# Lightning attention, then a Mish MLP, on one core: reordering the head, the k scalings and chunk 11's loads

## The chip, the cores and the metric

The kernel runs on one core of one Trainium2 chip. The metric is the device time of one execution in microseconds; a kernel's time is the median of several runs. The kernel before took 213.41 us, the median of three runs from 212.65 to 213.62. A smaller time is better. Chip engines are named as in the profile: PE is TensorE (PEld its weight loads), DVE VectorE, ACT ScalarE, POOL GpSimd, SP SyncE, which here only issues DMAs.

## The reference

Linear attention with a decay per head, in blocks of 64 positions, then a two-layer MLP whose activation is Mish, h * tanh(softplus(h)):

```python
# q, k, v: (4, 8, 768, 64); lam: (8,), 0.97 to 0.99
Dmask = np.where(rel >= 0, lam[:, None, None] ** rel[None, :, :], 0.0)
for b in range(nb):                       # 12 blocks of 64 positions
    intra = np.einsum('bhic,bhjc->bhij', qb, kb) * Dmask[None]
    intra = np.einsum('bhij,bhjd->bhid', intra, vb)
    inter = np.einsum('bhid,bhde->bhie', qb * lam_pow[None], kv_state)
    out[:, :, sl] = intra + inter
    kv_state = lam_block[None, :, None, None] * kv_state + np.einsum('bhsd,bhse->bhde', kb * rev_pow[None], vb)
x = out.transpose(0, 2, 1, 3).reshape(3072, 512)
h = x @ w_in                              # 512 -> 2048
g = h * np.tanh(softplus(h))
return g @ w_out                          # 2048 -> 512, fp32
```

## The kernel before

**Tiling.** The kernel works in chunks of 128 positions of one batch entry with all 8 heads: 6 positions times 4 entries make 24 chunks, numbered 0 to 23; a *group* is the four chunks of one position, so group n is chunks 4n to 4n+3 and 512 rows of the MLP. Heads stand in pairs j (0 to 3) with t = 0, 1 inside a pair. All matmuls take fp16 operands.

**A chunk's attention in groups 0 and 1.** `first_t` transposes k and q on TensorE (`pk`, `pq`, four matmuls each) and copies them to SBUF: `pkT` by ScalarE, `pqT` by VectorE. `first_s` makes the scores of the 8 heads (`pS`, eight matmuls into two tiles, t = 0 and 1), and VectorE multiplies each of the two tiles by its decay mask (`dm` in group 0, `maskT` in group 1) into `sb`. `first_o` multiplies `sb` by v (`pO`, eight matmuls; group 1 adds four with the state `wst`), and ScalarE copies the result into `xt`, the MLP's input for the group. Chunks of group 1 use k scaled by its decay, `ktil` (`scale_k`: VectorE in group 0 and the last group, GpSimd in the others), and q scaled by `lq`, which four exponentials of ScalarE make (`q_decays`). `wst` is cleared by `clear` and filled by `state_half` (`pv`, two chunks at a time).

**Groups 2 to 5.** k and q are transposed by DMA: `turn` scales k on GpSimd, and SyncE issues two DMA transposes, `qraw` and `kraw`. Two chunks at a time, `pair_s` makes the scores and the state's part of the outputs, `pair_o` the rest, and SyncE transposes the result (`xtok`) into `xt`. `pair_a` updates the state; the decay of the state (`wc`, L304) runs on GpSimd.

**The MLP.** First layer: `mm1_unit` makes 128 of the 2048 columns for all 512 rows of a group (four matmuls of 128x512, then Mish on ScalarE); in group 1 `mm1_tile` does 512 columns for one chunk at a time, so that it can follow the chunks. Second layer: `mm2_unit` is a quarter of the 2048 terms for one chunk, four matmuls of 128x512; every fourth is copied out of PSUM by ScalarE and stored. Called a *unit* below: four such matmuls.

**What sets the order.** The schedule is written out by hand: every engine runs its instructions in the order in which the code issues them, and semaphores hold them until their data are there. Tables named `steps` say after which unit a piece of attention is put in. The stages are: the head (setup and group 0's chunks, with fillers `busy`, matmuls on zeros); group 0's first layer, unit by unit, with chunk 4 and 5's attention put in; group 1's first layer by tiles `(chunk, s)`; then, for groups 0 and 1 together, 32 units of the second layer with group 2's pairs put in; then for each group 16 units of the first layer and 16 of the second.

**Loads.** q, k, v of chunks 1 to 23 and the weights are loaded by GpSimd's queue, fp32 to fp16, in the order of the code. From group 3 on they are held back behind a `tick` on GpSimd, a copy of one element that waits for a given output. GpSimd's own arithmetic stands in the same queue.

**PSUM.** `pk`, `pq`, `pO` and the first half of `pS` have one buffer each; `po` (also the second half of `pS`, and `pv`) and `ph` (also `busy`) have two.

Of the kernel before, what the change touches and what calls it, by code (L numbers as in the profile page):

```python
# [8 lines left out]
F16 = mybir.dt.float16  # L9
AF = mybir.ActivationFunctionType  # L10
ALU = mybir.AluOpType
# [9 lines left out]
def kernel(  # L21
# [183 lines left out]
    def first_t(c, m=0):  # L205

        out_ = []
        first = c < B
        for src, name in ((k0 if c == 0 else kn[c] if first else ktil[c], "pk"),
                          (q0 if c == 0 else qn[c], "pq")):  # L210
            pt = ps.tile([128, JP, C], F16, name=name, tag=name)
            for j in range(JP):
                nc.tensor.matmul(  # L213
                    pt[:, j, :], src[:, 2 * j : 2 * j + 2, :].rearrange("p h c -> p (h c)"), ident,
                    is_transpose=True, start=(j == 0), stop=(j == JP - 1),
                )
            out_.append(work.tile([128, JP, C], F16, name=f"{name}T", tag=f"{name}T", bufs=2))
            if name == "pk":
                nc.scalar.activation(out_[-1], pt, AF.Copy)
                busy(m)  # L220
            elif first:
                nc.vector.tensor_copy(out_[-1], pt)
            else:
                nc.vector.tensor_tensor(out=out_[-1], in0=pt, in1=lq, op=ALU.mult)
        kq[c] = out_

    def first_s(c):

        kT, qT = kq[c]
# [5 lines left out]
        sb0[c] = []  # L235
        for t in range(2):
            sb0[c].append(work.tile([128, JP, C], F16, name="sb", tag="sb", bufs=4))
            nc.vector.tensor_tensor(out=sb0[c][t], in0=pS[t],  # L238
                                    in1=dm[:, t] if c < B else bc(maskT, 1, JP), op=ALU.mult)

    def first_o(c):
# [13 lines left out]
        nc.scalar.activation(xt[n][:, :, b * C : (b + 1) * C], psO, AF.Copy)  # L255
# [201 lines left out]
    first_t(0, 2)  # L457
# [16 lines left out]
    nc.scalar.preload_act_table(AF.Mish)  # L474
    first_o(1)
    first_s(2)
    busy(3)
# [136 lines left out]
```

## Time and profile before

| what | value |
|---|---|
| median of three runs | 213.41 us (212.65 to 213.62) |
| the profiled execution's own time | 213.85 us |
| its span, first to last instruction | 212.1 us |
| TensorE busy | 203.5 us, 96% of the span |
| ScalarE, VectorE, GpSimd busy | 86.7, 67.6, 100.0 us |
| DMA on GpSimd's queue (loads) | 13.37 MB, 85.2% of the time of 16 engines |
| DMA on SyncE's queue (transposes) | 6.63 MB, 20.4% |

A row of the timeline has its start, its length, the engine, the line, the operation, the tiles (out<-in) and the count of instructions merged in it; in brackets stands the engine's idle time before it and what ended that. A row about DMA to landing gives the shortest, median and longest time from issue to the data's arrival. The chain is followed back from the last instruction, at each step to what released it. Ends of matmuls are modelled, so the length of a row of matmuls holds the last one's way through the array.

### The profile page before, as it was taken

What the parts mean: (1) busy time and instruction counts of PE and PEld (TensorE: products, weight loads), DVE (VectorE), ACT (ScalarE), POOL (GpSimd) and SP (SyncE); (2) the same over time, 40 slices, a digit from 0 to 9 for tenths busy, and PEclk for the clock granted to TensorE, in tenths of its full rate; (3) what the DMA queues carried; (4) which work ended last, traced back from release to release, by engine and by line L of the source; (5) the groups of instructions that cost most, each with busy time, mean ns of one, the idle gap of its engine ahead of it and who ended that gap; (6) DMA issues with size and microseconds to landing.
All of it is one profiled execution on the core that took longest, in us unless ns stands there. A gap on an engine that the chain in (4) does not pass through costs nothing.

```text
span 212.1 us, 4293 instructions
## 1 busy us (share of the span) xinstructions
PE 203.5 (96%) x1758; PEld 110.5 (52%) x1758; DVE 67.6 (32%) x124; ACT 86.7 (41%) x150; POOL 100.0 (47%) x143
## 2 busy tenths in 40 slices
PE   7989898999999899999999999999999999999994
PEld 4655446999745454445554454544444544444442
DVE  7686613725004442042440042482042510000000
ACT  4764575655421112346412356312456321566120
POOL 7997389932996348786965067921000000000000
PEclk9999999999999999999999999999999999999999
DMA  9999999999999999999997799997702032100112
GB/s 129 133 157 185 189 156 99 172 189 164 121 145 195 185 182 164 163 189 153 156 166 148 182 87 84 144 166 141 190 9 49 5 99 104 49 0 0 49 53 99
DMA packets 109895, 26.78 MB, mean 126 GB/s; under 512 B 102578, under 2 KB 106930, under 8 KB 109874
## 3 DMA queue, kind: packets, MB, share of 16 engines
q0 software_dynamic: 78080, 13.37, 85.2%
q1 hardware_dynamic: 27296, 6.63, 20.4%
q10 hardware_dynamic: 4498, 6.49, 9.9%
q8 instruction: 14, 0.23, 0.5%
q14 instruction: 7, 0.06, 0.1%
HBM read 27.26 MB, written 6.29 MB: 158 GB/s over the span
## 4 chain that ended last, share of the span: by engine, by line
PE 82%; DMA 9%; DVE 2%; ACT 1%; POOL 1%; issue 1%; SPq 1%; POOLq 0%; ACTq 0%; DVEq 0%
PE po L412 33%; PE ph L380 30%; DMA kraw<-ktil 7%; PE ph L398 7%; PE pO L253 2%; PE pS L324 2%; DMA kn<-in_k_dram 2%; PE pO L351 2%; PE pS L234 1%; PE pv L288 1%; PE pk L213 1%; SPq L272 1%; PE busy L167 1%; PE pq L213 1%; POOL vz L79 1%
## 5 line engine op out<-in xcount | busy, mean ns | idle before, releaser
L412 PE MATMUL po<-wout,hsg 128*128 128x512 f16 (+2 forms) x400 | 85.4, 371 | 0.0
L380 PE MATMUL ph<-xt,win 128*128 128x512 f16 (+2 forms) x328 | 73.0, 374 | 0.5 <-ACT xt L255 0.3
L387 ACT ACTIVATE hsg<-ph 128x512 f16<-128x512 f32 x80 | 47.7, 597 | 31.4 <-PE ph L380 31.1
L412 PEld LDWEIGHTS <-hsg 128*128 128x128 f16 x400 | 37.8, 98 | 42.3
L380 PEld LDWEIGHTS <-win 128*128 128x128 f16 x328 | 30.9, 98 | 36.3 <-issue 2.0
L427 ACT ACTIVATE osb<-po 128x512 f32<-128x512 f32 (+1 forms) x24 | 14.2, 593 | 74.8 <-PE po L412 69.9
L339 DVE TENSOR_TENSOR sb<-pS,maskT 128x512 f16<-128x512 f32 x32 | 19.9, 684 | 59.6 <-PE pS L324 59.6
L68 POOL DMA_DIRECT2D kn<-in_k_dram x23 | 21.0, 913 | 4.5 <-issue 1.9
L76 POOL DMA_DIRECT2D qn<-in_q_dram x23 | 20.9, 907 | 4.6 <-DMA wout<-in_moe_w_out_dram 3.0
L79 POOL DMA_DIRECT2D vz<-in_v_dram x24 | 21.7, 908 | 2.4 <-DMA win<-in_moe_w_in_dram 1.6
L263 POOL TENSOR_TENSOR ktil<-kn,lk 128x512 f16<-128x512 f16 x16 | 16.7, 1054 | 2.5 <-DMA kn<-in_k_dram 2.3
L398 PE MATMUL ph<-xt,win 128*128 128x128 f16 x256 | 15.6, 219 | 0.7 <-ACT xt L255 0.7
L357 DVE TENSOR_TENSOR xtok<-pO,lqt 128x512 f16<-128x512 f32 x16 | 10.3, 687 | 15.5 <-PE pO L351 15.5
L398 PEld LDWEIGHTS <-win 128*128 128x128 f16 x256 | 14.5, 98 | 1.1 <-issue 0.8
L304 POOL TENSOR_TENSOR wc<-raws,lbc 128x512 f16<-128x512 f32 x8 | 8.6, 1096 | 9.8 <-DVE raws L303 5.4
L402 ACT ACTIVATE hsg<-ph 128x512 f16<-128x512 f32 x16 | 9.6, 597 | 7.5 <-PE ph L398 7.5
L421 DVE COPY osb<-po 128x128 f32<-128x128 f32 x1 | 0.3, 291 | 38.7 <-PE po L412 38.7
L368 POOL COPY tick<-hsg 1x1 f16<-1x1 f16 x25 | 4.4, 178 | 12.5 <-ACT hsg L387 12.4
L167 PE MATMUL busy<-kzero 128*128 128x512 f16 x16 | 6.6, 505 | 1.2 <-DVE kzero L149 1.2
L253 PE MATMUL pO<-sb,vz 128*128 128x128 f16 x64 | 6.4, 230 | 0.4 <-DVE sb L238 0.3
L238 DVE TENSOR_TENSOR sb<-pS,maskT 128x512 f16<-128x512 f32 x8 | 5.2, 687 | 5.1 <-PE pS L234 5.1
L263 DVE TENSOR_TENSOR ktil<-kn,lk 128x512 f16<-128x512 f16 (+1 forms) x8 | 6.5, 849 | 0.0
(71 smaller groups left out, 115.9 us busy)
## 6 DMA issues: line engine op xcount, KB each, us to landing
out_dram<-osb ACTq DMA_DIRECT2D x23, 256.0 KB, 2.6
vz<-in_v_dram POOLq DMA_DIRECT2D x24, 128.0 KB, 4.4
kn<-in_k_dram POOLq DMA_DIRECT2D x23, 128.0 KB, 5.2
qn<-in_q_dram POOLq DMA_DIRECT2D x23, 128.0 KB, 4.8
wout<-in_moe_w_out_dram POOLq DMA_DIRECT2D x4, 512.0 KB, 10.4
win<-in_moe_w_in_dram POOLq DMA_DIRECT2D x3, 512.0 KB, 9.9
kn<-in_k_dram SPq DMA_DIRECT2D x1, 256.0 KB, 3.4
qn<-in_q_dram ACTq DMA_DIRECT2D x1, 256.0 KB, 4.1
```

Source lines behind the costliest of these rows:

```text
L68: nc.gpsimd.dma_start(out=kn[i], in_=chunk_rows(k, i))
L76: nc.gpsimd.dma_start(out=qn[i], in_=chunk_rows(q, i))
L79: nc.gpsimd.dma_start(out=vz[i % NVB][:, :, 0:D], in_=chunk_rows(v, i))
L253: nc.tensor.matmul(psO[:, j, :], vf[:, o : o + 128], sb0[c][t][:, j, :], start=(n == 0 and t == 0), stop=(t == 1))
L263: (nc.vector if i < B or i >= (NG - 1) * B else nc.gpsimd).tensor_tensor(out=t, in0=kn[i], in1=bc(lk, 2, D), op=ALU.mult)
L339: nc.vector.tensor_tensor(out=s.sb[x][t], in0=pS[x][t], in1=bc(maskT, 1, JP), op=ALU.mult)
L357: nc.vector.tensor_tensor(out=xtok[:, :, :, t, :], in0=s.pO[t], in1=bc(bc(lqj[:, :, t], 1, 2), 3, D), op=ALU.mult)
L380: nc.tensor.matmul(ph_t[ni][:, lo:hi], win_t(ni, kc), xt[n][:, kc, lo:hi], start=(kc == 0), stop=(kc == NKC - 1))
L387: nc.scalar.activation(hsg[n][:, ni, :], ph_t.pop(ni), AF.Mish)
L398: nc.tensor.matmul(ph[:, u, :], win_t(w * s + u, kc), xt[n][:, kc, b * C : (b + 1) * C], start=(kc == 0), stop=(kc == NKC - 1),)
L412: nc.tensor.matmul(po[:, lo:hi], hsg[n][:, ki, b * C : (b + 1) * C], wout[part][:, kk, lo:hi], start=(ki == 0), stop=(ki == NKI - 1),)
L427: nc.scalar.activation(o, i, AF.Copy)
```

## The change

The program has the same instructions before and after, on every engine; their order changes.

- In the head, `first_t`, `first_s` and `first_o` are split into pieces (k and q; scores and each mask; outputs and their copy). Chunk 1's scores stand ahead of chunk 0's outputs; chunk 1's q^T copy stands between chunk 0's two masks, and chunk 2's between chunk 1's two. The exponentials for `lq` and the load of the Mish table come earlier on ScalarE. The fillers are spread otherwise, 16 in all as before.
- `clear(1)` to `clear(3)` come later on VectorE, and `scale_k` of chunks 2 and 3 before the first layer's units instead of after the second.
- Chunk 4's transposes and scores come one unit earlier, chunk 5's scores before group 1's first tile, chunk 7's outputs one tile later.
- On GpSimd, chunk 5 is scaled before chunk 7's k is loaded; chunk 11's k and q are loaded ahead of group 1's state decays, and chunk 8's `turn` stands between these.
- In the second layer of groups 0 and 1 the first pair's scores come after unit 9 (was 11), its outputs after 13 (was 14), the second pair's scores after 16 (was 17).

VectorE, the head; `pqT` is the copy of q^T, `sb` a masked score tile, in the order of chunks, two a chunk. Before:

```order
L222 COPY pqT_195<-pq_190 128x512
L449 MEMSET wst_162 128x256
L238 TENSOR_TENSOR sb_214<-pS_204,dm_157 128x512
L238 TENSOR_TENSOR sb_216<-pS_205,dm_157 128x512
L222 COPY pqT_231<-pq_226 128x512
L449 MEMSET wst_162 128x256
L238 TENSOR_TENSOR sb_261<-pS_251,dm_157 128x512
L238 TENSOR_TENSOR sb_263<-pS_252,dm_157 128x512
L222 COPY pqT_282<-pq_277 128x512
```

And in the change:

```order
L224 COPY pqT_195<-pq_190 128x512
L472 MEMSET wst_162 128x256
L248 TENSOR_TENSOR sb_218<-pS_208,dm_157 128x512
L224 COPY pqT_232<-pq_227 128x512
L248 TENSOR_TENSOR sb_234<-pS_209,dm_157 128x512
L248 TENSOR_TENSOR sb_249<-pS_239,dm_157 128x512
L224 COPY pqT_273<-pq_268 128x512
L248 TENSOR_TENSOR sb_276<-pS_240,dm_157 128x512
```

Each of the second and third q^T copies now stands between the two masks of the chunk before, and the second and third memsets have gone from here.

VectorE, the state update of group 0 (`ktil` of chunks 0 to 3, then `wst`). Before:

```order
L263 TENSOR_TENSOR ktil_377<-kn0_98,lk_158 128x512
L263 TENSOR_TENSOR ktil_379<-kn_103,lk_158 128x512
L295 TENSOR_TENSOR wst_162<-pv_428,lbc_160 64x8x64 x2
L263 TENSOR_TENSOR ktil_447<-kn_112,lk_158 128x512
L263 TENSOR_TENSOR ktil_449<-kn_117,lk_158 128x512
L295 TENSOR_TENSOR wst_162<-pv_463,lbc_160 64x8x64 x2
```

And in the change:

```order
L286 TENSOR_TENSOR ktil_374<-kn0_98,lk_158 128x512
L286 TENSOR_TENSOR ktil_376<-kn_103,lk_158 128x512
L472 MEMSET wst_162 128x256
L286 TENSOR_TENSOR ktil_379<-kn_112,lk_158 128x512
L286 TENSOR_TENSOR ktil_381<-kn_117,lk_158 128x512
L318 TENSOR_TENSOR wst_162<-pv_430,lbc_160 64x8x64 x2
L318 TENSOR_TENSOR wst_162<-pv_461,lbc_160 64x8x64 x2
```

Chunks 2 and 3 are scaled before the first `wst` product, with the last memset ahead of them.

GpSimd, from the second wout load to chunk 8 and 9's scaling (`kn_413` is chunk 8's k, `kn_1071` chunk 11's; `wc` are group 1's decays). Before:

```order
L107 DMA wout1_84<-in_moe_w_out_dram 128x4x512
L263 TENSOR_TENSOR ktil_409<-kn_398,lk_158 128x512
L107 DMA wout2_85<-in_moe_w_out_dram 128x4x512
L107 DMA wout3_86<-in_moe_w_out_dram 128x4x512
L68 DMA kn_413<-in_k_dram 128x8x64
L76 DMA qn_415<-in_q_dram 128x8x64
L68 DMA kn_618<-in_k_dram 128x8x64
L76 DMA qn_620<-in_q_dram 128x8x64
L68 DMA kn_622<-in_k_dram 128x8x64
L76 DMA qn_624<-in_q_dram 128x8x64
L304 TENSOR_TENSOR wc00_163<-raws_938,lbc_160 128x512
L304 TENSOR_TENSOR wc10_165<-raws_977,lbc_160 128x512
```

which is followed by chunk 11's k and q and the scalings of chunks 8 and 9. In the change, from chunk 10's k on (`kn_632`; chunk 11's is `kn_636`):

```order
L68 DMA kn_632<-in_k_dram 128x8x64
L76 DMA qn_634<-in_q_dram 128x8x64
L68 DMA kn_636<-in_k_dram 128x8x64
L76 DMA qn_638<-in_q_dram 128x8x64
L327 TENSOR_TENSOR wc00_163<-raws_936,lbc_160 128x512
L286 TENSOR_TENSOR ktil_940<-kn_415,lk_158 128x512
L327 TENSOR_TENSOR wc10_165<-raws_981,lbc_160 128x512
L286 TENSOR_TENSOR ktil_1075<-kn_628,lk_158 128x512
```

Chunk 11's two loads have moved ahead of both decays, and chunk 8's scaling between them. The diff:

```diff
-    def first_t(c, m=0):
-
...
-            out_.append(work.tile([128, JP, C], F16, name=f"{name}T", tag=f"{name}T", bufs=2))
-            if name == "pk":
-                nc.scalar.activation(out_[-1], pt, AF.Copy)
-                busy(m)
-            elif first:
-                nc.vector.tensor_copy(out_[-1], pt)
-            else:
-                nc.vector.tensor_tensor(out=out_[-1], in0=pt, in1=lq, op=ALU.mult)
-        kq[c] = out_
-    def first_s(c):
-
...
+    def turn_pe(c, name):
+
+        src = (k0 if c == 0 else kn[c] if c < B else ktil[c]) if name == "pk" else (q0 if c == 0 else qn[c])
...
+        kq[c, name] = work.tile([128, JP, C], F16, name=f"{name}T", tag=f"{name}T", bufs=2)
+        return kq[c, name], pt
+
+    def first_k(c):
+        to, pt = turn_pe(c, "pk")
+        nc.scalar.activation(to, pt, AF.Copy)
+
+    def first_q(c):
+        to, pt = turn_pe(c, "pq")
+        if c < B:
+            nc.vector.tensor_copy(to, pt)
+        else:
+            nc.vector.tensor_tensor(out=to, in0=pt, in1=lq, op=ALU.mult)
+
+    def first_t(c):
+        first_k(c)
+        first_q(c)
+
+    score = {}
+    outs = {}
+
+    def scores(c):
+
+        kT, qT = kq[c, "pk"], kq[c, "pq"]
...
-        sb0[c] = []
-        for t in range(2):
-            sb0[c].append(work.tile([128, JP, C], F16, name="sb", tag="sb", bufs=4))
-            nc.vector.tensor_tensor(out=sb0[c][t], in0=pS[t],
-                                    in1=dm[:, t] if c < B else bc(maskT, 1, JP), op=ALU.mult)
-
-    def first_o(c):
+        score[c] = pS
+        sb0[c] = [None, None]
+
+    def masks(c, t):
+        sb0[c][t] = work.tile([128, JP, C], F16, name="sb", tag="sb", bufs=4)
+        nc.vector.tensor_tensor(out=sb0[c][t], in0=score[c][t],
+                                in1=dm[:, t] if c < B else bc(maskT, 1, JP), op=ALU.mult)
+
+    def first_s(c):
+        scores(c)
+        masks(c, 0)
+        masks(c, 1)
+
...
-                                 kq[c][1][:, j, :], start=True, stop=False)
+                                 kq[c, "pq"][:, j, :], start=True, stop=False)
...
-        nc.scalar.activation(xt[n][:, :, b * C : (b + 1) * C], psO, AF.Copy)
+        outs[c] = psO
+
+    def copy_out(c):
+        n, b = divmod(c, B)
+        nc.scalar.activation(xt[n][:, :, b * C : (b + 1) * C], outs[c], AF.Copy)
+
+    def first_o(c):
+        outputs(c)
+        copy_out(c)
...
@@ -454,29 +477,36 @@
     decays(1)
     nc.vector.tensor_copy(q0, qn[0])
     nc.scalar.activation(dm[:, 0], dm[:, 0], AF.Exp)
-    first_t(0, 2)
+    first_k(0)
+    busy(2)
+    first_q(0)
     clear(0)
     nc.scalar.activation(dm[:, 1], dm[:, 1], AF.Exp)
     nc.scalar.activation(lk, lnb, AF.Exp, scale=ek)
     nc.scalar.activation(lqt, lnb, AF.Exp, scale=eq)
     nc.scalar.activation(lbc, lnp, AF.Exp, scale=float(C))
-    busy(1)
-    first_s(0)
-    first_t(1)
-    clear(1)
     q_decays()
     busy(1)
-    first_o(0)
-    first_s(1)
-    busy(3)
+    scores(0)
+    masks(0, 0)
+    first_t(1)
+    masks(0, 1)
+    nc.scalar.preload_act_table(AF.Mish)
+    busy(1)
+    scores(1)
+    masks(1, 0)
+    outputs(0)
     first_t(2)
+    copy_out(0)
+    masks(1, 1)
+    busy(2)
+    first_s(2)
+    first_o(1)
+    clear(1)
+    busy(2)
+    first_t(3)
     clear(2)
-    nc.scalar.preload_act_table(AF.Mish)
-    first_o(1)
-    first_s(2)
-    busy(3)
-    first_t(3)
-    clear(3)
+    busy(2)
     first_s(3)
     first_o(2)
     busy(2)
@@ -485,14 +515,17 @@
     mm1_part(0, 1, 0, GT - C)
     scale_k(0)
     scale_k(1)
+    clear(3)
+    scale_k(2)
+    scale_k(3)
     for i in range(B, NVB - 2):
         load_chunk(i)
     load_k(NVB - 2)
     scale_k(B)
     load_q(NVB - 2)
     load_v(NVB - 2)
+    scale_k(B + 1)
     load_k(NVB - 1)
-    scale_k(B + 1)
     load_q(NVB - 1)
     scale_k(B + 2)
     load_v(NVB - 1)
@@ -503,14 +536,11 @@
     load_wout(3)
     load_k(2 * B)
     load_q(2 * B)
-    steps = {12: ((first_t, 4),), 14: ((first_s, 4),), 15: ((first_t, 5), (first_o, 4))}
+    steps = {11: ((first_t, 4),), 13: ((first_s, 4),), 14: ((first_t, 5),), 15: ((first_o, 4), (first_s, 5))}
     for u in range(NKI):
         mm1_unit(0, u)
         if u in (1, 3):
             state_half(0, u // 2, "po")
-        if u == 1:
-            scale_k(2)
-            scale_k(3)
         if u == 6:
             nc.vector.tensor_scalar(out=maskT, in0=rel, scalar1=0.0, scalar2=None, op0=ALU.is_ge)
         if u in (6, 7, 8, 10):
@@ -518,21 +548,20 @@
             nc.vector.memset(vz[i][:, :, D : 2 * D], 0.0)
         for f, c in steps.get(u, ()):
             f(c)
-    c = 2 * B
-    for f, i in ((load_k, c + 1), (load_q, c + 1), (load_k, c + 2), (load_q, c + 2)):
-        f(i)
-    steps = {(4, 0): ((first_s, 5), (first_t, 6)), (4, 1): ((first_o, 5), (first_s, 6)),
-             (4, 2): ((first_t, 7),), (4, 3): ((first_o, 6), (first_s, 7)), (5, 0): ((first_o, 7),),
-             (6, 1): ((state_half, 0),), (6, 2): ((state_half, 1),)}
+    g = 2 * B
+    for c in (g + 1, g + 2, g + 3):
+        load_k(c)
+        load_q(c)
+    steps = {(4, 0): ((first_t, 6),), (4, 1): ((first_o, 5), (first_s, 6)), (4, 2): ((first_t, 7),),
+             (4, 3): ((first_o, 6), (first_s, 7)), (5, 1): ((first_o, 7),),
+             (6, 1): ((state_half, 0), (turn, g)), (6, 2): ((state_half, 1),)}
     for c in range(B, 2 * B):
         for s in range(WS):
             mm1_tile(c, s)
             for f, i in steps.get((c, s), ()):
                 f(*((1, i, "po") if f is state_half else (i,)))
-    c = 2 * B
-    for f, i in ((load_k, c + 3), (load_q, c + 3), (turn, c), (turn, c + 1), (load_v, c),
-                 (turn, c + 2), (load_v, c + 1), (turn, c + 3), (load_v, c + 2), (load_v, c + 3)):
-        f(i)
+    for f, i in ((turn, 1), (load_v, 0), (turn, 2), (load_v, 1), (turn, 3), (load_v, 2), (load_v, 3)):
+        f(g + i)
 
     for n in range(NT - 1, NG):
         dense = [(mm2_unit, m, b, part) for m in ((0, 1) if n < NT else (n,))
@@ -550,7 +579,7 @@
                 s = Pair()
                 s.n, s.b = n + 1, b
                 pairs.append(s)
-            steps = (((11, pair_s, 0), (14, pair_o, 0), (17, pair_s, 1), (20, pair_o, 1),
+            steps = (((9, pair_s, 0), (13, pair_o, 0), (16, pair_s, 1), (20, pair_o, 1),
                       (24, pair_a, 1)) if n < NT else
                      ((4, pair_s, 0), (8, pair_o, 0), (13, pair_s, 1), (17, pair_o, 1),
                       (20, pair_a, 1)))
```

More of the change, by code (lines that the diff above doesn't have):

```diff
@@ L203 @@
     sb0 = {}
[L205 to L229 removed]
+    def turn_pe(c, name):
+        src = (k0 if c == 0 else kn[c] if c < B else ktil[c]) if name == "pk" else (q0 if c == 0 else qn[c])
+        pt = ps.tile([128, JP, C], F16, name=name, tag=name)
+        for j in range(JP):
+            nc.tensor.matmul(
+                pt[:, j, :], src[:, 2 * j : 2 * j + 2, :].rearrange("p h c -> p (h c)"), ident,
+                is_transpose=True, start=(j == 0), stop=(j == JP - 1),
+            )
+        kq[c, name] = work.tile([128, JP, C], F16, name=f"{name}T", tag=f"{name}T", bufs=2)
[16 more added lines that the diff above has]
+        kT, qT = kq[c, "pk"], kq[c, "pq"]
         pS = [ps.tile([128, JP, C], F32, name="pS", tag=("pS", "po")[t], bufs=1 + t) for t in range(2)]
@@ L234, in first_s, with outputs @@
                 nc.tensor.matmul(pS[t][:, j, :], kT[rs, j, :], qT[rs, j, :], start=True, stop=True)
[L235 to L241 removed]
+        score[c] = pS
[8 more added lines that the diff above has]
+        masks(c, 1)
+    def outputs(c):
         n, b = divmod(c, B)
```

## The prediction

> **What bounds the kernel now.** I read the page's busy shares first, then TensorE's waits, then the timeline of each stretch in which TensorE waits, and last the loads and transposes that end those waits, with their landings.
>
> ```profile
> span 212.1 us, 4293 instructions
> PE 203.5 (96%) x1758; PEld 110.5 (52%) x1758; DVE 67.6 (32%) x124; ACT 86.7 (41%) x150; POOL 100.0 (47%) x143
> ```
>
> TensorE sets the end. The change removes no matmul and adds none, so it can only win idle time of TensorE. Where that lies, the timeline's rows below say in brackets (idle time, and what ended it): in the head, at one state update, at the hand-over to group 1, and at two k transposes by DMA. The bracket is shorter than the time lost, because a matmul's recorded end trails the start of the next; so I take losses from start to start.
>
> **The head.** Its rows, of all engines; each `x8` of pS is one chunk's scores.
>
> ```profile
> 8.19 0.63 PE L213 MATMUL pq<-ident,qn 128*128 128x128 f16 x4
> 8.44 0.60 ACT L219 ACTIVATE pkT<-pk 128x512 f16<-128x512 f16 x1 [1.36 <-PE pk L213]
> 8.93 1.26 ACT L196 ACTIVATE lq<-ei,lnp 128x128 f32<-128x128 f32 x4
> 9.05 1.14 PE L253 MATMUL pO<-sb,vz 128*128 128x128 f16 x8
> 9.14 0.41 DVE L222 COPY pqT<-pq 128x512 f16<-128x512 f16 x1
> 9.56 0.27 DVE L449 MEMSET wst<- 128x256 uint32 x1
> 10.12 0.41 PE L234 MATMUL pS<-pqT,pkT 64*128 64x128 f16 x8
> 10.56 1.29 DVE L238 TENSOR_TENSOR sb<-pS,dm 128x512 f16<-128x512 f32 x2 [0.73 <-PE pS L234]
> 12.21 1.28 ACT L474 ACT_TABLE_LOAD   x1
> 12.38 0.40 PE L234 MATMUL pS<-pqT,pkT 64*128 64x128 f16 x8
> 14.65 0.40 PE L234 MATMUL pS<-pqT,pkT 64*128 64x128 f16 x8 [0.67 <-ACT pkT L219]
> 16.28 0.81 PE L380 MATMUL ph<-xt,win 128*128 128x384 f16 x4 [0.25 <-ACT xt L255]
> ```
>
> Scores of chunks 1, 2 and 3 start at 10.12, 12.38 and 14.65. Chunk 1's stand behind chunk 0's outputs (9.05), which wait for both masks. Chunk 3's wait for a k^T copy that stands behind the Mish table's 1.28 us.
>
> After the change pq of chunk 1 still ends at 8.82 (8.19 + 0.63). VectorE copies it at once, 0.41, so the scores of chunk 1 can start at 9.3, 0.8 earlier. The second mask of chunk 0 (1.29 / 2 = 0.65) moves behind that copy, to 9.95, and holds chunk 0's outputs until then. The lq exponentials (1.26) move into the 1.36 us in which ScalarE waited, and the table load behind chunk 1's k^T copy, 9.04 to 10.3. Chunk 2's k^T copy is needed at 10.9, so both are covered; without the cover each would delay a k^T copy by 1.3. Chunk 0's outputs are copied to xt behind it, until 12.1, by 0.1 before chunk 1's outputs ask for the one pO buffer.
>
> From there VectorE is the limit. Outputs of chunk 0 run to about 10.5, pk and pq of chunk 2 to 11.1, its q^T copy to 11.6: scores of chunk 2 at 11.6 (0.8 earlier). Then three masks (1.95), a memset (0.27) and the next q^T copy (0.41) follow on VectorE to 14.2: scores of chunk 3 at 14.2, their k^T copied by 14.1 with no table load ahead. That is **0.4** earlier, and the first ph (16.28) comes 0.4 earlier as well.
>
> **Bounds behind the head.** Rows of TensorE, VectorE and the loads that come next:
>
> ```profile
> 19.29 1.89 PE L380 MATMUL ph<-xt,win 128*128 128x512 f16 x8
> 20.74 1.29 DVE L263 TENSOR_TENSOR ktil<-kn,lk 128x512 f16<-128x512 f16 x2
> 21.48 0.32 PE L288 MATMUL pv<-vz,ktil 128*64 128x64 f16 x8 [0.30 <-DVE ktil L263]
> 22.09 0.32 PE L288 MATMUL pv<-vz,ktil 128*64 128x64 f16 x8 [0.29 <-DVE ktil L263]
> 22.33 1.04 PE L380 MATMUL ph<-xt,win 128*128 128x512 f16 x4
> ...
> L95 POOL DMA_DIRECT2D win<-in_moe_w_in_dram x3: 833/842/850, 13.1 to 14.6; - x3
> ...
> DMA to landing us min/median/max: 8.1/9.9/11.7
> ...
> 27.27 1.04 POOL L263 TENSOR_TENSOR ktil<-kn,lk 128x512 f16<-128x512 f16 x1 [2.35 <-DMA kn<-in_k_dram]
> 30.11 0.39 PE L213 MATMUL pk<-ident,ktil 128*128 128x128 f16 x4
> 35.56 1.05 PE L398 MATMUL ph<-xt,win 128*128 128x128 f16 x16 [0.69 <-ACT xt L255]
> 44.11 0.22 PE L253 MATMUL pO<-sb,vz 128*128 128x128 f16 x1 [0.26 <-DVE sb L238]
> 55.61 9.23 PE po L412 x43
> ```
>
> A 128x512 matmul starts every 0.215 us (9.23 / 43), so a unit of four takes 0.86.
>
> State update of group 0: eight ph from 19.29 end at 21.0; pv starts at 21.48 and, after a half of 0.2, again at 22.09: 0.9 lost, since ktil of chunks 2 and 3 stands behind the wst products. After, the masks of chunk 3 end at 15.95; four ktil (0.65 each) and the moved memset (0.27) end at 18.8, before pv is reached at 20.6. Gain **0.9**, together 1.3; uncovered it would be the same wait as now.
>
> But the loads don't move. The first issue of L95, win1, lands at 13.1 + 8.1 = 21.2, and unit 4 would ask for it at 22.33 - 1.3 = 21.0: 0.2 given back. Then chunk 4's transposes, moved one unit up, would come at 30.11 - 0.86 - 1.1 = 28.15, while their ktil ends at 27.27 + 1.04 = 28.3: 0.2 given back, **0.9** left. So it hardly matters whether the head itself wins 0.4 or nothing.
>
> Hand-over: TensorE stood 0.7 before 35.56 for chunk 4's copy into xt. Scores of chunk 5 (0.33 by starts) now lie in that wait: **+0.3**. Chunk 7's outputs waited at 44.11, about 0.4 by starts, for a mask one tile (0.9) behind its scores; they get a second tile between: **+0.4**. Scaling chunk 5 before loading chunk 7 on GpSimd costs chunk 7's load 1 us of a wait of some 4; it is used at 38.6 or later: nothing. The second matmul stage starts at 55.6 - 1.65 = **53.95**.
>
> **The pairs of group 2.** Rows of GpSimd, of the wout loads and the k transposes with their landings, of the chain (64.83: the last k transpose of group 2), and of TensorE:
>
> ```profile
> 46.32 0.88 POOL L76 DMA_DIRECT2D qn<-in_q_dram  x1 [3.04 <-DMA wout<-in_moe_w_out_dram]
> 51.25 1.04 POOL L304 TENSOR_TENSOR wc<-raws,lbc 128x512 f16<-128x512 f32 x1 [4.05 <-DVE raws L301]
> 55.41 2.06 POOL L263 TENSOR_TENSOR ktil<-kn,lk 128x512 f16<-128x512 f16 x2
> ...
> L107 POOL DMA_DIRECT2D wout<-in_moe_w_out_dram x2: 750/780/811, 37.3 to 38.1; - x2
> ...
> DMA to landing us min/median/max: 10.6/11.5/12.4
> ...
> L272 SPq DMA_TRANSPOSE kraw<-ktil x16: 1188/1247/2387, 56.5 to 152.1; - x16
> ...
> DMA to landing us min/median/max: 2.4/2.9/8.5
> ...
> 64.83 8.52 DMA kraw<-ktil
> 65.90 0.62 PE L324 MATMUL pS<-qraw,kraw 64*128 64x128 f16 x16
> 72.44 0.40 PE L324 MATMUL pS<-qraw,kraw 64*128 64x128 f16 x8
> 73.40 0.40 PE L324 MATMUL pS<-qraw,kraw 64*128 64x128 f16 x8 [0.56 <-DMA kraw<-ktil]
> 92.75 0.40 PE L324 MATMUL pS<-qraw,kraw 64*128 64x128 f16 x8 [0.49 <-DMA kraw<-ktil]
> ```
>
> GpSimd's qn at 46.32 waited for a wout load issued eight loads before it. If that is a limit of eight loads in flight, chunk 11's k and q, now issued straight behind it, wait for the third and fourth wout, which land at 37.3 + 10.6 = 47.9 and 38.1 + 12.4 = 50.5. Behind them on GpSimd stand the group-1 decays wc and ktil of chunk 8, and SyncE's transposes wait for those. So the q load runs 50.9 to 51.85, wc to 52.9, ktil of chunk 8, now between the two wc, starts at 52.95 instead of 55.41: 2.45 earlier. wc itself comes 0.6 later than at 51.25; the first pair asks for it at 62.6. SyncE issued its transposes in order, the k of chunk 8 at 56.5, the k of chunk 11 at 64.83; six issues of some 1.25 us and one longer fill that, so chunk 11's k transpose is issued 2.45 earlier too, at 62.4; with the same 8.52 us it lands at **70.9**.
>
> TensorE now wants it earlier. Stage start 53.95, ten units (8.65), first pair: 62.6 (65.90 before). From the first pair's scores to the last chunk's was 73.40 - 0.7 - 65.90 = 6.8 without the wait (0.7: second half due at 72.44 + 0.23 = 72.67), with three units each side of the outputs; now it is four and three: 7.65. Chunk 11's scores are due at 70.25 and run at 70.95, **0.7 of waiting**. At this point 15 units are left, where 14 were at 73.40, so the gain is 73.40 - 70.95 - 0.86 = **1.6**.
>
> Behind it TensorE has the same distances as before (outputs at unit 20, next pairs at unit 4 of the next group), and SyncE's and GpSimd's work hangs on TensorE's outputs; the wait at 92.75 moves along, and no later row shows one. Sum: 0.4 + 0.9 - 0.4 + 0.3 + 0.4 = 1.6 (1.65 unrounded) before the pairs, 1.6 behind them.
>
> **The numbers.** The profiled execution took 213.85 us, 1.75 around its span of 212.1; with 1.6 less, 212.25. It is 0.44 above the median, so against 213.41 I predict **211.8 us**, a span of 210.5. Less than 0.5% (1.07 us) can't be told from no change.
>
> **Rivals.**
>
> Transposes in time (15%): chunk 11's k lands by 70.25. For it: the median of the k transposes is 2.9, and 7.8 would do. Against it: this group's loads, outputs and transposes are all under way at once, and chunk 11's loads now travel with the first transposes. Gain 73.40 - 70.25 - 0.86 = 2.3: 211.1.
>
> Transposes bound by the queue (15%), the slower side: if chunk 11's k^T lands when it did, at 73.35, issuing it earlier buys nothing, and a pair moved up a unit has one unit more behind its wait: 0.86 lost, 214.3. It costs from a landing after 72.5. For it: the first k transpose is issued at 56.5 and the last lands at 73.35, 17 us for seven transposes, so the queue may be full. Against it: it would need 11 us from issue, and the 8.52 is the most of all 16. The Trainium skill (DMA: Bandwidth & Descriptors, on arbitration) says each DMA engine takes turns between its queues packet by packet; by that rule the added loads slow the transposes in flight, and the landing would slip towards this case.
>
> Half of it given back (12%): landing 71.5 to 72.5, gain 1.0 to 0, 212.9.
>
> The clock (8%): three fillers before the scores take 1.46 us early and 0.82 later.
>
> ```profile
> 1.18 1.46 PE L167 MATMUL busy<-kzero 128*128 128x512 f16 x3 [1.18 <-DVE kzero L149]
> 10.46 0.82 PE L167 MATMUL busy<-kzero 128*128 128x512 f16 x3
> ```
>
> TensorE reaches full rate between them. If chunk 0's later outputs put that off by 3 us, some 2.5 us of matmuls take twice as long, 0.4 of it inside waits. TensorE is then past the loads' bounds (no 0.4 given back) and 1.7 later at the pairs than forecast, beyond the 0.7 of waiting: gain 0.6, 212.8. The Trainium skill (TensorE: Matmul & The Clock Gate, Part 1) has a free-running window of about 3.4 us that must be busy; the rows agree on the two rates, and the only new gap that I see, 0.2 us at 9.8, is short against it.
>
> The forecast keeps 50%. Faster by over 0.5% gets nearly all of the forecast's share, the first rival's and a little of the clock's: 0.60; slower by over 0.5% needs a landing after 73.6: 0.08; within: 0.32. The range takes in the first rival and stops inside the slower one: 210.7 to 213.6.
>
> **What will show it.** Right: pv without a wait near 20.6; unit 4 starting when win1 lands; chunk 4's transposes right behind ktil; one wait for kraw of 0.3 to 1 us near 70.9. Wrong: kn or qn of chunk 11 issued before 47.9; kraw landing past 72; pS of chunk 2 not before 12; three fillers still at the slow rate after 11 us.

## The result, and the profile after

The changed kernel took **211.57 us**, the median of 21 runs (210.19 to 213.55); the kernel before, run beside it, 213.28 (21 runs, 212.23 to 216.95). The ratio is **0.9918, 95% interval 0.9896 to 0.9940**: faster by 0.8%, 1.7 us. The forecast was 211.8, in a range from 210.7 to 213.6. The profiled execution of the changed kernel took 212.0, and its span is 210.2, 1.85 below before's. Here and below a median holds all runs of a kernel, while a ratio leaves out the few that were disturbed.

The head, in the timeline of the changed kernel (start, length, engine, line; the idle time before a row in brackets):

```profile
8.90 0.42 DVE L224 COPY pqT<-pq 128x512 f16<-128x512 f16 x1 [0.23 <-PE pq L210]
9.09 1.28 ACT L494 ACT_TABLE_LOAD   x1
9.38 0.40 PE L242 MATMUL pS<-pqT,pkT 64*128 64x128 f16 x8 [0.26 <-DVE pqT L224]
9.71 0.81 PE L268 MATMUL pO<-sb,vz 128*128 128x128 f16 x8
10.81 0.59 PE L167 MATMUL busy<-kzero 128*128 128x512 f16 x2
10.85 0.60 ACT L219 ACTIVATE pkT<-pk 128x512 f16<-128x512 f16 x1 [0.47 <-PE pk L210]
11.01 0.42 DVE L224 COPY pqT<-pq 128x512 f16<-128x512 f16 x1 [0.49 <-PE pq L210]
11.50 0.40 PE L242 MATMUL pS<-pqT,pkT 64*128 64x128 f16 x8
14.04 0.40 PE L242 MATMUL pS<-pqT,pkT 64*128 64x128 f16 x8
15.68 0.81 PE L403 MATMUL ph<-xt,win 128*128 128x384 f16 x4 [0.25 <-ACT xt L274]
```

Scores of chunks 1, 2 and 3 start at 9.38, 11.50 and 14.04 (10.12, 12.38 and 14.65 before), and the first ph 0.6 earlier. No k^T copy waits behind the table load. Two fillers at 10.81 take 0.59, the fast rate. VectorE stood 0.49 before chunk 2's q^T copy at 11.01, so it was not what held that chunk's scores: its copy ended at 11.43 and ScalarE's k^T copy at 11.45, each started when TensorE's transposes had ended.

Then the state update, chunk 4's transposes, the hand-over to group 1 and the start of the second layer:

```profile
19.75 1.90 PE L403 MATMUL ph<-xt,win 128*128 128x512 f16 x8 [1.15 <-DMA win<-in_moe_w_in_dram]
21.58 0.44 PE L311 MATMUL pv<-vz,ktil 128*64 128x64 f16 x16
22.30 7.08 PE L403 MATMUL ph<-xt,win 128*128 128x512 f16 x32 [0.28 <-ACT hsg L410]
28.35 1.04 POOL L286 TENSOR_TENSOR ktil<-kn,lk 128x512 f16<-128x512 f16 x1 [2.36 <-ACT hsg L410]
29.45 0.40 PE L210 MATMUL pk<-ident,ktil 128*128 128x128 f16 x4
...
35.76 1.05 PE L421 MATMUL ph<-xt,win 128*128 128x128 f16 x16 [0.35 <-ACT xt L274]
...
54.78 2.54 PE L435 MATMUL po<-wout,hsg 128*128 128x512 f16 x11
```

Both waits of pv for ktil are gone: all sixteen run in one piece. But 1.15 us now pass in front of unit 2, for the third piece of w_in's first quarter. The chain of waits has its load: issued at 12.37, it takes 7.33 us. Chunk 4's k, loaded behind w_in, landed at 28.20; GpSimd scaled it from 28.35 to 29.39 (the row's bracket names an `hsg` that ended at about the same time), and chunk 4's transposes start at 29.45, 0.2 later than the units before them allow (22.30 + 6.92, what 32 such matmuls take in the kernel with two loads out, is 29.22).

```profile
12.37 7.33 DMA win<-in_moe_w_in_dram
```

The second layer starts at 54.78, where 55.44 was the start before (the prediction's row at 55.61 is the chain's, which counts the first matmul from the end of the record before it). That is 0.66 earlier. The pairs of group 2, on GpSimd, SyncE and TensorE:

```profile
48.57 0.87 POOL L68 DMA_DIRECT2D kn<-in_k_dram  x1 [1.69 <-DMA wout<-in_moe_w_out_dram]
51.38 0.88 POOL L76 DMA_DIRECT2D qn<-in_q_dram  x1 [1.94 <-PE ph L421]
52.27 1.05 POOL L327 TENSOR_TENSOR wc<-raws,lbc 128x512 f16<-128x512 f32 x1
53.27 1.04 POOL L286 TENSOR_TENSOR ktil<-kn,lk 128x512 f16<-128x512 f16 x1
...
54.34 1.20 SPq L295 DMA_TRANSPOSE kraw<-ktil  x1
63.70 1.84 SPq L295 DMA_TRANSPOSE kraw<-ktil  x1
...
63.51 0.62 PE L347 MATMUL pS<-qraw,kraw 64*128 64x128 f16 x16
70.91 0.86 PE L347 MATMUL pS<-qraw,kraw 64*128 64x128 f16 x16
90.69 0.62 PE L347 MATMUL pS<-qraw,kraw 64*128 64x128 f16 x16
```

Sixteen scores without a wait last 0.62; those at 70.91 last 0.86, so chunk 11's half, which begins at 71.38 (70.91 + 0.23 + 0.24), lost 0.24 where 0.73 was lost before (73.40 - 72.44 - 0.23). At 90.69 there is no wait; before, 0.66 went there (92.75 - 91.86 - 0.23, the first start from the same view of before).

**Where the span went.** In every profile of this study, before's, the changed kernel's and twelve variants', the rest of the time is fixed. Let S be the start of the second layer. From S to chunk 11's scores it takes 17.23 us when no transpose is late (counted as if the pairs stood in their old places: where they stand a unit earlier, 0.86 is added), and from there to the end 138.0. What is late adds P, lost at the pairs of group 2, and W, lost at the scores of group 3's first pair (89 to 93 us). So span = S + 155.2 + P + W, to within 0.2 in all fourteen. Before: 55.44 + 155.2 + 0.73 + 0.66 = 212.0. After: 54.78 + 155.2 + 0.24 = 210.2. The 1.85 are 0.66 of S, 0.5 of P and 0.66 of W. A profile is one execution, though, and the executions of one kernel lie 1 us and more apart; so medians decide below, and S, P and W say only where one execution stood.

### The profile page after: what moved, and what is told of

It reads as the page before. It is cut to its first block, busy times and chain, and to the rows that moved or that the text cites. A ratio compares the mean times of both kernels' runs of the same rounds, so it can differ in the third digit from the quotient of the medians.

```text
span 210.2 us, 4290 instructions
## 1 busy us (share of the span) xinstructions
PE 202.7 (96%) x1758; PEld 109.8 (52%) x1758; DVE 67.6 (32%) x124; ACT 86.6 (41%) x150; POOL 99.7 (47%) x143
## 4 chain that ended last, share of the span: by engine, by line
PE 88%; POOL 6%; DMA 3%; ACT 1%; issue 1%; DVE 0%; POOLq 0%
PE po L435 40%; PE ph L403 32%; PE ph L421 7%; DMA win<-in_moe_w_in_dram 3%; PE pS L347 2%; PE pO L374 2%; POOL vz L79 2%; POOL kn L68 1%; POOL qn L76 1%; PE pv L311 1%; PE pO L353 1%; PE pO L268 1%; POOL win L92 1%; ACT hsg L410 1%; PE pk L210 1%
## 5 line engine op out<-in xcount | busy, mean ns | idle before, releaser
L450 ACT ACTIVATE osb<-po 128x512 f32<-128x512 f32 (+1 forms) x24 | 14.2, 593 | 74.3 <-PE po L435 68.7
L274 ACT ACTIVATE xt<-pO 128x512 f16<-128x512 f32 x8 | 4.8, 596 | 3.4 <-PE pO L268 3.1
```

The lines of the kernel that those rows point to most:

```text
L450: nc.scalar.activation(o, i, AF.Copy)
```

## The experiments

Three theories. **Additive**: each part wins what the prediction gave it, whatever the others do. **Landings**: what the head, the scalings and the steps win is held up by the next transfer to land (w_in, then the k transposes of chunks 9, 11 and 13), so that parts don't add. **Chunk 11**: the gain stands or falls with chunk 11's earlier loads. The medians come with the ratio to the kernel before in the same call (213.3 to 213.6).

| kernel | S | P | W | span | its own time | median (runs) | ratio, 95% interval |
|---|---|---|---|---|---|---|---|
| before | 55.44 | 0.73 | 0.66 | 212.1 | 213.85 | 213.28 (21) | |
| after | 54.78 | 0.24 | 0 | 210.2 | 212.00 | 211.57 (21) | 0.9918 (0.9896 to 0.9940) |
| head alone | 55.17 | 1.00 | 0 | 211.4 | 213.16 | 212.70 (12) | 0.9958 (0.9932 to 0.9984) |
| scalings alone | 54.72 | 0.84 | 0 | 210.8 | 212.68 | 213.09 (12) | 0.9976 (0.9946 to 1.0006) |
| loads alone | 55.16 | 0 | 0 | 210.4 | 212.26 | 212.41 (10) | 0.9935 (0.9906 to 0.9964) |
| pairs alone | 55.34 | 0.61 | 0 | 211.2 | 212.96 | 213.36 (12) | 1.0015 (0.9990 to 1.0041) |
| after, old head | 54.48 | 0.21 | 0.72 | 210.6 | 212.42 | 211.08 (6) | 0.9875 (0.9836 to 0.9915) |
| after, old scalings | 53.83 | 1.26 | 0 | 210.3 | 212.24 | 211.71 (8) | 0.9930 (0.9899 to 0.9961) |
| after, old loads | 53.49 | 0.73 | 0 | 209.4 | 211.21 | 211.56 (11) | 0.9912 (0.9878 to 0.9945) |
| after, old pairs | 53.94 | 1.36 | 0 | 210.5 | 212.31 | 212.02 (12) | 0.9915 (0.9883 to 0.9947) |
| after, old steps | 56.01 | 0.26 | 0.38 | 211.9 | 213.79 | 211.38 (7) | 0.9913 (0.9885 to 0.9941) |
| after, old head and pairs | 53.83 | 0 | 0 | 209.1 | 210.85 | 210.82 (6) | 0.9878 (0.9846 to 0.9910) |
| before, two loads out | 55.00 | 0 | 0 | 210.4 | 212.14 | 213.72 (12) | 1.0016 (0.9988 to 1.0043) |
| after, two loads out | 53.19 | 0 | 0 | 208.6 | 210.37 | 210.37 (6) | 0.9866 (0.9823 to 0.9908) |

**The head alone** is the kernel before with the new head; the same lines undone give "old head" below.

```diff
-    busy(1)
-    first_s(0)
-    first_t(1)
-    clear(1)
     q_decays()
...
+    scores(0)
+    masks(0, 0)
+    first_t(1)
+    masks(0, 1)
+    nc.scalar.preload_act_table(AF.Mish)
...
```

> The kernel before with the head's new order alone (split pieces, lq and Mish table moved, fillers spread as in the change). Theory of bounds (loads and k transposes land when they land, and TensorE's gain ahead of one passes only as far as the landing allows): the first ph comes 0.4 to 0.6 us earlier, and 0 to 0.6 us of that is left at the end: 212.7 to 213.3 against 213.3 before. Theory of sums (each idle stretch that is removed passes to the end whole): 0.6 us faster, 212.7.

212.70, 0.4% faster, which both theories allow. In its profile the first ph comes at 15.35 and waits there 0.36 and at 17.30 another 0.68 for w_in; both waits of pv stay, and P is 1.00.

**The loads alone**: chunk 11's k and q ahead of the decays, chunk 8's `turn` between these.

```diff
-    for c in (g + 1, g + 2):
+    for c in (g + 1, g + 2, g + 3):
...
-             (6, 1): ((state_half, 0),), (6, 2): ((state_half, 1),)}
+             (6, 1): ((state_half, 0), (turn, g)), (6, 2): ((state_half, 1),)}
...
-    for f, i in ((load_k, 3), (load_q, 3), (turn, 0), (turn, 1), (load_v, 0), (turn, 2), (load_v, 1), (turn, 3), (load_v, 2), (load_v, 3)):
+    for f, i in ((turn, 1), (load_v, 0), (turn, 2), (load_v, 1), (turn, 3), (load_v, 2), (load_v, 3)):
```

> The kernel before with chunk 11's k and q loaded ahead of group 1's decays and chunk 8's turn between these, and nothing else. If the last k transpose of group 2 lands by its issue: it lands about 2 us earlier, the wait at 73.4 us goes, TensorE is otherwise as before: 0.6 to 0.7 us faster, 212.6. If the transposes are bound by their queue: it lands at 73.3 as before and the time is 213.3.

212.41, 0.65% faster (1.0 us between the medians, 1.4 by the ratio), the largest share that one part has alone and one and a half to two times what was expected. Its timeline shows chunk 11's k transpose issued early, and no wait left behind the second layer's start:

```profile
53.84 1.19 SPq L295 DMA_TRANSPOSE kraw<-ktil  x1
63.08 1.26 SPq L295 DMA_TRANSPOSE kraw<-ktil  x1
...
72.16 0.62 PE L347 MATMUL pS<-qraw,kraw 64*128 64x128 f16 x16
90.83 0.62 PE L347 MATMUL pS<-qraw,kraw 64*128 64x128 f16 x16
```

**The head, and the loads, undone** in the changed kernel.

> The changed kernel with the head's old order. Theory of bounds: as fast as the changed kernel within 0.2 us (211.6 to 211.8), since the win loads hold TensorE back in either. Theory of sums: 0.6 us slower than it, 212.2.

211.08: not slower than the changed kernel, if anything faster. The new head is not needed for the gain. (Its profiled execution, 212.42, was its slowest by far: the other five took 210.53 to 211.13.)

> The changed kernel with chunk 11's loads and chunk 8's turn back behind group 1's decays. By the prediction the last k transpose is issued about 1.7 us later than in the changed kernel and lands near 73, TensorE waits for it some 1.5 to 2 us from 70.9: 1.3 us slower than the changed kernel, 212.9 to 213.2. If issuing it earlier buys nothing: as the changed kernel, 211.6.

211.56, the same as the changed kernel: the expected loss did not come. The timeline says why. With its loads in the old order, GpSimd's decays and scalings ran

```profile
49.30 1.04 POOL L327 TENSOR_TENSOR wc<-raws,lbc 128x512 f16<-128x512 f32 x1 [2.92 <-DVE raws L324]
50.65 1.04 POOL L327 TENSOR_TENSOR wc<-raws,lbc 128x512 f16<-128x512 f32 x1 [0.31 <-DVE raws L324]
51.63 0.94 POOL L68 DMA_DIRECT2D kn<-in_k_dram  x1
52.56 0.88 POOL L76 DMA_DIRECT2D qn<-in_q_dram  x1
53.45 2.05 POOL L286 TENSOR_TENSOR ktil<-kn,lk 128x512 f16<-128x512 f16 x2
```

The decays wait for `raws`, thus for TensorE's state update. TensorE comes 1.95 earlier in this execution (S 53.49 against 55.44), and ktil of chunk 8 comes 1.96 earlier as well (53.45 against 55.41): what the old order cost is mostly made up by the other parts. So "chunk 11" falls as the one cause: its loads win 1.0 to 1.4 us by themselves and nothing that can be seen on top of the rest (the interval would hide some 0.7 us).

**The pairs alone**, and undone:

```diff
-            steps = (((11, pair_s, 0), (14, pair_o, 0), (17, pair_s, 1), (20, pair_o, 1),
+            steps = (((9, pair_s, 0), (13, pair_o, 0), (16, pair_s, 1), (20, pair_o, 1),
```

> The kernel before with group 2's pairs in their new places alone (scores after units 9 and 16, outputs after 13 and 20). The last k transpose of group 2 is issued as before and lands near 73.3 us; TensorE reaches it one unit earlier and waits 0.86 us longer, with one more unit behind the wait: 0.9 us slower than before, 214.2. If moving the pairs pays by itself (their outputs and the next group's transposes come earlier): 213.3 or less.

213.36, no change; the 0.86 us of loss were not there. Chunk 11's transpose, issued at 65.01 where it was 64.83 before, landed at 71.71 instead of 73.35, ahead of its use; chunk 9's was late instead:

```profile
64.07 0.40 PE L347 MATMUL pS<-qraw,kraw 64*128 64x128 f16 x8
64.91 0.40 PE L347 MATMUL pS<-qraw,kraw 64*128 64x128 f16 x8 [0.45 <-DMA kraw<-ktil]
72.09 0.62 PE L347 MATMUL pS<-qraw,kraw 64*128 64x128 f16 x16
```

> The changed kernel with group 2's pairs in their old places (scores after units 11 and 17, outputs after 14 and 20). Theory of bounds: TensorE comes to the last k transpose one unit later, finds it landed, and loses no 0.2 to 0.7 us there: as fast as the changed kernel or up to 0.5 us faster, 211.1 to 211.6. If the new places pay: slower than 211.6 by up to 0.9.

212.02 as the median of all runs, but 0.9915 as a ratio, which is 211.5: the same as the changed kernel. In the profiled execution chunk 11 waited 1.21 for a transpose issued at 64.44.

**The scalings undone** (chunks 2 and 3 scaled after unit 1 again) and **alone**:

```diff
     scale_k(1)
     clear(3)
-    scale_k(2)
-    scale_k(3)
...
+        if u == 1:
+            scale_k(2)
+            scale_k(3)
```

> The changed kernel with the k scaling of chunks 2 and 3 back behind the second unit. Theory of bounds: pv waits 0.9 us again, but the win loads, which hold unit 2 or unit 4 in the changed kernel, have that much longer to land: 0 to 0.5 us slower than the changed kernel, 211.6 to 212.1. Theory of sums: 0.9 us slower, 212.5.

211.71. Both waits of pv are back (0.29 each), but this execution had no wait for w_in, and S is 53.83, earlier than in the changed kernel; then 1.08 (1.26 from start to start) went at chunk 9's transpose, which landed at 64.00.

> The kernel before with chunks 2 and 3 scaled ahead of the first layer's units, nothing else. Theory A (each part wins the idle time of TensorE that it removes): pv has no wait, 0.9 us of start-to-start loss gone; the loads of win give back little, since TensorE comes no earlier than in the kernel before by more than 0.9: unit 4 due at 21.4 against win1's landing between 20.9 and 22.9 in the profiles so far; the pairs of group 2 come up to 0.9 us earlier against a chunk 11 k transpose that lands unmoved: all of it waits at 73.4. Theory B (what is won ahead of the transpose of chunk 11 is taken back there unless its loads move): 213.3, within 0.3 of the kernel before, with a wait of about 1.4 us for kraw instead of 0.56. Theory A alone: 212.4.

213.09: 0.24% faster, an interval that just takes in no change. In its profile the pv run in one piece, unit 2 waits 0.31 for w_in, and P is 0.84. S gained 0.72 on the kernel before and the kraw wait remained; this is nearer to "landings" than to the 212.4 of "additive".

**The steps undone** (chunk 4's and 5's transposes and scores, chunk 7's outputs where they were):

```diff
-    steps = {11: ((first_t, 4),), 13: ((first_s, 4),), 14: ((first_t, 5),), 15: ((first_o, 4), (first_s, 5))}
+    steps = {12: ((first_t, 4),), 14: ((first_s, 4),), 15: ((first_t, 5), (first_o, 4))}
...
-             (4, 3): ((first_o, 6), (first_s, 7)), (5, 1): ((first_o, 7),),
+             (4, 3): ((first_o, 6), (first_s, 7)), (5, 0): ((first_o, 7),),
```

> The changed kernel with group 1's attention in its old places among the units and tiles (chunk 4's transposes after unit 12, chunk 5's scores behind the first tile, chunk 7's outputs after tile (5, 0)). The waits of 0.7 before group 1's first tile and 0.4 before chunk 7's outputs come back, and chunk 4's transposes no longer follow its scaling closely (0.2 won): 0.5 us slower than the changed kernel, 212.1, if that passes to the end; 211.6 if the k transposes of group 2 hold TensorE back by as much.

211.38, not slower. Its profiled execution was its slowest by far (213.79; the other six took 211.12 to 211.50): the waits before chunk 4's tile (0.69) and chunk 7's outputs (0.26) are back as expected, and 1.84 went at unit 2 for a w_in load that took 7.92 us from the same issue time.

```profile
12.36 7.92 DMA win<-in_moe_w_in_dram
```

**Fewer bytes ahead of w_in.** None of the undone parts cost anything that can be seen (each interval is 0.6 to 0.9 us wide to either side), so whether landings hold the rest was asked directly: v of chunks 2 and 3 is not loaded (these chunks multiply by v of chunks 0 and 1), in the kernel before and in the changed one, and GpSimd issues the loads of w_in about 1.75 us earlier.

```diff
-    for f, i in ((load_v, 0), (load_k, 2), (load_q, 2), (load_v, 1), (load_k, 3), (load_q, 3),
-                 (load_v, 2), (load_v, 3)):
+    for f, i in ((load_v, 0), (load_k, 2), (load_q, 2), (load_v, 1), (load_k, 3), (load_q, 3)):
...
-        vf = vz[c].rearrange("p h c -> p (h c)")
+        vf = vz[c % 2 if c < B else c].rearrange("p h c -> p (h c)")
```

> Leaves out the loads of v of chunks 2 and 3 in the kernel before; these two chunks take v of chunks 0 and 1. GpSimd issues the loads of w_in behind them two issues (1.74 us) earlier. Theory A (landings bound the changed kernel's head, VectorE and ScalarE that of the kernel before): win lands about 1.7 us earlier, but the kernel before had no wait for win; its waits for ktil of chunks 2 and 3 stay. At most the wait for chunk 11's transpose goes (0.7): 212.6 to 213.4. Theory B (loads bound neither): 213.3 as before.

213.72, ratio 1.0016: nothing won. (Its profiled execution was the fastest of its twelve.)

> Leaves out the same two loads in the changed kernel. Theory A (landings of w_in hold what its head wins): the wait for win at 19.75 (1.15 us) and the one at unit 4 go, chunk 4's transposes come by 28.2, and the stage of the second layer starts at 53.6 or earlier; 0.4 to 1.2 us below the changed kernel: 210.4 to 211.2, and the distance to the kernel before with the same loads left out is 1.9 us or more. Theory B (loads bound neither): 211.6 as the changed kernel, the distance between the two 1.7 us as before.

210.37, 1.2 below the changed kernel, and 3.35 below the kernel before with the same loads out, where 1.7 lay between the two with all loads. Its timeline has no wait for w_in, nor any for ktil or hsg:

```profile
18.76 1.89 PE L404 MATMUL ph<-xt,win 128*128 128x512 f16 x8
20.57 0.44 PE L312 MATMUL pv<-vz,ktil 128*64 128x64 f16 x16
20.95 7.08 PE L404 MATMUL ph<-xt,win 128*128 128x512 f16 x32
27.87 0.39 PE L211 MATMUL pk<-ident,ktil 128*128 128x128 f16 x4
```

and TensorE's waits are down to four (engine, line, what was waited for; us in total, times, longest):

```profile
PE busy L168 <- DVE kzero L148: 1.2, 1, 1.2
PE ph L422 <- ACT xt L275: 0.4, 1, 0.4
PE ph L404 <- ACT xt L275: 0.3, 1, 0.3
PE pk L211 <- ACT lnp L476: 0.2, 1, 0.2
```

So loads hold back the changed kernel and not the kernel before: between the two kernels lie 0.8% with all loads and 1.5% without these two, and the 0.7% of difference is a little more than the intervals leave to chance (0.55%, taken together). The changed kernel's interval and this one's overlap only from 0.9896 to 0.9908. That the load is w_in's is what the profiles say, where the wait stands at w_in; the run itself does not separate it, since every later load comes earlier too (the last wout lands at 47.54, in the changed kernel at 50.84).

**A version with fewer parts**: the changed kernel with the old head and the old places of the pairs, which keeps the scalings, the steps and the loads.

> The changed kernel with the head in the old order and the pairs of group 2 in their old places (what is left: the k scalings, chunk 4, 5 and 7's steps, chunk 5's scaling, chunk 11's loads and chunk 8's turn). Without the head 211.08 was measured, without the pairs 212.02, the changed kernel 211.57. Theory A (parts add up by what each lost or won when it was taken out): 211.57 - 0.5 + 0.45 = 211.5. Theory B (head and pairs only shift waits to the next landing): 211.1 to 211.9, the same as the changed kernel, with TensorE's waits moved between win and the k transposes of group 2. Theory C (the head is needed for the gain): 212.0 or more.

210.82 (six runs, 210.42 to 211.69), ratio 0.9878: the lowest median of those that compute everything. Its profile has no late transpose behind the second layer's start. In group 0's first layer unit 2 starts at 18.83, 0.08 behind the landing of its weights at 18.75, so the old, later head loses nothing there; what is left is 0.26 for hsg:

```profile
18.83 1.89 PE L403 MATMUL ph<-xt,win 128*128 128x512 f16 x8
20.64 0.44 PE L311 MATMUL pv<-vz,ktil 128*64 128x64 f16 x16
21.34 7.08 PE L403 MATMUL ph<-xt,win 128*128 128x512 f16 x32 [0.26 <-ACT hsg L410]
...
64.28 0.62 PE L347 MATMUL pS<-qraw,kraw 64*128 64x128 f16 x16
70.82 0.62 PE L347 MATMUL pS<-qraw,kraw 64*128 64x128 f16 x16
```

It beats the kernel before. That it beats the changed kernel as well is likely but not shown: the intervals, 0.9846 to 0.9910 and 0.9896 to 0.9940, overlap.

## Why the prediction was right, and where its steps were wrong

**Right**: the time (211.57 for 211.8) and the sign; the gain of 1.7 for 1.6. Not all of the steps behind it were.

- **The head**: forecast 9.3, 11.6, 14.2 for the scores and 0.4 won; measured 9.38, 11.50, 14.04 and 0.6. The table load was covered, as worked out. "From there VectorE is the limit" was not so for chunk 2, as its idle time at 11.01 shows, and for chunk 3 VectorE, free at 13.50, waited for nothing but a transpose that ended at 13.52: a tie. The 0.6 is also in part luck: TensorE came to its fast rate at another moment in each execution. The filler behind chunk 1's transposes took 0.63 at 8.62 before, the slow rate, 0.47 at 8.66 after, and 0.38 at 8.19 with the head alone. The first ph came between 15.82 and 16.28 in the seven profiles with the old head, before's being the latest, and between 15.26 and 15.75 in the seven with the new one; the means differ by 0.45, about the forecast.
- **"It hardly matters whether the head itself wins 0.4 or nothing"**: right. With the old head the time was 211.08. The head helps alone (212.70 against 213.44) and, as far as can be seen, not with the rest.
- **The scalings**: ktil of chunks 2 and 3 no longer holds pv; 0.9 of start-to-start loss removed, as forecast. What follows it was wrong.
- **"But the loads don't move … 0.2 given back" twice**: the first of the two failed. It took a landing read from one execution, 21.2, for a fixed point, and looked at w_in's second quarter only. The third piece of its first quarter, which landed at 18.03 before, landed at 19.70 here and cost 1.15 at unit 2; behind it the second quarter landed at 22.25. Up to S the profiled execution won 0.66 instead of 1.65. In other executions with the new head it landed at 17.60 and 18.41 and cost nothing (S 53.49 with the old loads, 53.83 with the old scalings; the forecast's 53.95 is 53.8 when counted from 55.44). The order of instructions is not what moves it: the changed kernel and those with the old loads, the old pairs and the old steps issue the same ones up to 20 us, and it landed at 19.70, 17.60, 18.89 and 20.28. The second 0.2, at chunk 4's transposes, came as forecast, though 1.1 us later than forecast: ktil ended at 29.39, for 28.3. So the forecast of S lies within what executions show, but its bound was not one.
- **The hand-over**: +0.3 and +0.4. The wait ahead of group 1's first tile fell from 0.69 to 0.35 and that at chunk 7's outputs (0.26) went, as forecast. The time without these steps, 211.38, shows no loss (0.6 would be hidden); 0.7 that is won ahead of late transposes need not reach the end.
- **Eight loads in flight**: kn and qn of chunk 11 were issued at 48.57 and 51.38, behind the third and fourth wout, which landed at 48.01 and 50.84 (the bracket at 51.38 names another releaser), and ktil of chunk 8 at 53.27, for 52.95. Right.
- **Chunk 11's transpose**: landing 71.33 for 70.9, lost 0.24 for 0.7. The issue came at 63.70 instead of 62.4 (SyncE took 9.36 from the k of chunk 8 to that of chunk 11, where the forecast kept 8.33), and the transpose took 7.6, not 8.5. TensorE came 0.9 later than forecast, which hid most of it.
- **"The wait at 92.75 moves along"**: failed. It vanished, and it is absent from ten of the twelve variants' profiles, also from those in which only one part was put into the kernel before. It comes and goes with the execution, and that of before had it. It made about 0.66 of the 1.85 by which the spans differ; that the forecast's sum fits this span is luck: what it overrated up to S, 1.0, is about what it missed at the pairs (0.5) and here (0.66).
- **The slower rival's price**: its 0.86 rested on chunk 11's landing staying where it was. With the pairs alone moved it landed 1.64 earlier from a later issue, and the time did not change. Chunk 11's landing was not held back by the added loads either: with the loads alone the transpose took 5.8 us from issue, the shortest with all loads. The Trainium skill (DMA: Bandwidth & Descriptors, Queues, rings and completion order, on arbitration) has queues taking turns on each engine, by which the added loads would slow it; the measurement says that for this transpose this was not what decided. For chunk 8's k transpose the direction agrees: it took 4.9 to 6.2 us in the eight profiles with chunk 11's loads ahead and 2.6 to 4.2 in the six without (2.84 before, 6.09 after, so that it landed at 60.44, 1.1 later than before, from an issue 2.2 earlier). There chunk 8's q transpose was still under way as well, so that the runs don't say which of the two slowed it. **The clock**: refuted for this execution by the fillers at 10.81, which run at the fast rate behind chunk 0's later outputs.
- **What an undone part would cost**: my expectation for the kernel without the early loads (slower by 1.3 or more) failed; in its profile the reason is that it priced them at the old pace of TensorE, on whose outputs the decays ahead of the old loads wait.

What stays open: how the gain divides in a typical execution. By their ratios head, scalings, loads and pairs alone sum to 0.9 + 0.5 + 1.4 - 0.3 = 2.5 us, without the steps, which were not run alone; together all five gave 1.75. That the parts overlap is likely but not shown: the sum of the four is sure only to some 1.2 us by their intervals, and profiles of single executions can't tell it, as their waits for w_in and kraw come and go.

## What to carry to other kernels

A landing time out of one trace is a sample and not a bound: before idle time of the bounding engine is counted as won, ask by how much the next transfer misses and how far its landing moves from one execution to the next. If taking out any one part of a change costs nothing, the parts may share a bound behind them; take the suspected transfer away in both versions and see which of them moves. The fewest parts that reach that bound may be the better kernel: here three of the five gave 210.82.

## What the runs showed of the hardware

Loads that were issued at the same time, within 0.03 us, landed up to 2.7 us apart: the third piece of w_in's first quarter, issued at 12.36 to 12.39 by GpSimd, landed between 17.60 and 20.28 in the profiles that load everything, in 5.2 to 7.9 us. The k transpose of chunk 11 took 5.7 us (two loads out), 5.8 (loads alone), 6.7 (pairs alone), 7.6 (after) and 8.5 (before) from issue to landing. I had taken both as properties of the order; these numbers are as large as the effect that was forecast. A third thing moved with the execution, the moment from which TensorE's matmuls run at the fast rate: the last slow one starts between 6.6 and 10.1 us in the fourteen profiles (9.87 before, 8.66 after). With the same old head the first ph came up to 0.46 us apart, and latest in the two executions, before's and that of the pairs alone, in which that moment came latest.
